# Bias load to the POOL queue, one load for W1's first block, a later parameter transpose, and the last store in partition halves

## The chip, the cores and the metric

The kernel runs on one core of one Trainium2 chip. The metric is device time in microseconds, the median of several executions. The span inside the profile is about 1.3 µs shorter than the run's time.

## The reference, cut to what matters

`x` is 2048 × 640 in bf16. The output is `g * a + (1 - g) * b`, where `g` is a sigmoid gate per row, `a` a diagonal complex state-space layer (640 states, a scan over 2048 steps, projections in and out) and `b` an MLP.

```python
h = jnp.einsum("bsd,df->bsf", x, w1) + b1     # 640 -> 1728
h = _gelu(h)
b = jnp.einsum("bsf,fd->bsd", h, w2) + b2     # 1728 -> 640
Lam_bar = jnp.exp(jnp.exp(log_dt) * Lam)
y = 2.0 * jnp.einsum("blp,dp->bld", hseq, Cmat).real + x * Dskip
```

## The kernel before

A small scheduler inside the kernel orders operations per engine by priority (a lower number goes first). What matters here is the start and the end.

At the start, SP loads a part of `x` (`xna`), W1 in row blocks, and a transposed part of `x`; ACT loads five small parameter rows into the tile `rows`. TensorE (PE) runs some dummy matmuls, transposes `xna` (line 413), starts the first 40 first-layer matmuls (line 621: five row blocks of W1 times eight column blocks), and puts in between one transpose of `rows` (line 432), which needs all five rows. The next stage begins with line 641.

```python
load("xna", "sp", "l_xna", xn[0][:, :, 0:KN * 128], x2[0:512, 0:KN * 128].rearrange(...), ["xna"], 0, ...)
for h in range(2):                                   # W1's first row block, two loads
    fs = slice(h * FW // 2, (h + 1) * FW // 2)
    load(f"w1_0{h}", "sp", f"l_w10{h}", W1sb[:, 0, fs], B_w1[0:128, fs], [("w1", 0, h)], 0.1 + h, ...)
w1load(1, "sp", 1.3)
w1load(2, "sp", 2)
xtrans(0, range(KN, KD), 3, 1.8)                     # x, transposed by the DMA
# ... cut ...
load("b1b", "act", "l_b1b", rows[RT:RT + 1, :]..., B_b1[nmain:F]..., ["b1b"], prio=-96, dur=0.4)
# ... cut ...
op("cols", "pe", 0.3, list(ROWS) + ["b1b", "ident"], [("bank", 7)], f_cols, prio=9.5)
```

At the end, the last block of 128 output rows is finished by VectorE (DVE) in two column parts, and each part is stored from SP as soon as it is ready. The last part has 256 columns (512 B per row).

```python
def f_st(hf=hf, cols=cols):
    return dma_inc("sp", nc.sync.dma_start(o2[c * 128:(c + 1) * 128, cols], osb[c % NO][:, cols]), f"stl{hf}")
op(f"stl{hf}", "sp", 0.5, [("osb", c % NO, hf)], [], f_st, prio=1000 + c, lat=2.5)
```

Of the kernel before, what the change touches and what calls it, by code (L numbers as in the profile page):

```python
# [147 lines left out]
class Prog:  # L148
# [8 lines left out]
    def op(self, name, eng, dur, reads, writes, fn, prio=None, lat=0.0, after=()):  # L157
        deps = {}
        for k in reads:
            for w in self.last_w.get(k, ()):  # L160
                deps[w.idx] = w
        for k in writes:
            for w in self.last_w.get(k, ()):
                deps[w.idx] = w
            for r in self.last_r.get(k, ()):
                deps[r.idx] = r
        for a in after:
            deps[a.idx] = a
        deps = list(deps.values())
        E = self.E  # L170

        def run(eg, deps=deps, eng=eng, fn=fn):
            E.wait(eng, *[d.done for d in deps if not (eng == "pe" and d.eng == "pe")])
            return fn()

        it = self.sch.add(name, eng, dur, deps, run, prio=prio, lat=lat)
        for k in writes:
            self.last_w[k] = [it]
            self.last_r[k] = []
        for k in reads:  # L180
            self.last_r.setdefault(k, []).append(it)
        return it


def bass_gated_mix__ssm_conv_s5__dense_activation_gelu__prompt_kernel(
# [18 lines left out]
    _, S, D = A_x.shape  # L204
# [18 lines left out]
    o2 = out[0]  # L223
    TWO_PI = 2.0 * math.pi

    with ExitStack() as es:
# [80 lines left out]
        def dma_inc(eng, ins, sem):  # L307
            SEM(sem)
            E.count.setdefault(sem, 0)
            ins.then_inc(sems[sem], 16)  # L310
            E.count[sem] += 16
            return (sem, E.count[sem])
# [7 lines left out]
        def d_mm(n):  # L320
            return n / 2400.0 + 0.004


        def load(name, eng, sem, dst, src, writes, prio, dur=0.5, lat=2.5, reads=(), **kw):
            def fn():
                return dma_inc(eng, engines[eng].dma_start(dst, src), sem)  # L326
            return op(name, eng, dur, reads, writes, fn, prio=prio, lat=lat)
# [22 lines left out]
        def w1load(k, eng, prio):  # L350
            load(f"w1_{k}", eng, f"l_w1{k}", W1sb[:, k, 0:FW], B_w1[k * 128:(k + 1) * 128, 0:FW], [("w1", k)], prio=prio, lat=2.6)
# [1 line left out]
        KN = 2  # L353

        load("xna", "sp", "l_xna", xn[0][:, :, 0:KN * 128], x2[0:512, 0:KN * 128].rearrange("(c p) d -> p c d", p=128), ["xna"], 0, dur=0.45, lat=2.0)
        for h in range(2):
            fs = slice(h * FW // 2, (h + 1) * FW // 2)
            load(f"w1_0{h}", "sp", f"l_w10{h}", W1sb[:, 0, fs], B_w1[0:128, fs], [("w1", 0, h)], 0.1 + h, dur=0.45, lat=2.0)
        w1load(1, "sp", 1.3)
        w1load(2, "sp", 2)  # L360
        xtrans(0, range(KN, KD), 3, 1.8)
# [13 lines left out]
        for i, (nm, (r0, src)) in enumerate(ROWS.items()):  # L375
            src = src.rearrange("(k p) -> k p", p=128)
            load(nm, "act", "l_" + nm, rows[r0:r0 + src.shape[0], :], src, [nm], prio=-100 + i, dur=0.4)
        load("b1b", "act", "l_b1b", rows[RT:RT + 1, :].rearrange("o (a p) -> o a p", a=2),
             B_b1[nmain:F].rearrange("(o p) -> o p", o=1).unsqueeze(1).broadcast_to([1, 2, FL]), ["b1b"], prio=-96, dur=0.4)

        def f_iota():
            inc("pool", nc.gpsimd.iota(io_i[:, :], pattern=[[1, 128]], base=0, channel_multiplier=-1))  # L382
# [48 lines left out]
        def f_cols():  # L431
            return inc("pe", nc.tensor.transpose(psC, rows[:, :], ident[:, :]))  # L432

        op("cols", "pe", 0.3, list(ROWS) + ["b1b", "ident"], [("bank", 7)], f_cols, prio=9.5)

        def f_cols1():
            return inc("dve", nc.vector.tensor_copy(out=cols[:, :], in_=psC[:, 0:RT + 1]))
# [147 lines left out]
        def pe_prio():  # L585
            ctr["pe"] += 1
            return ctr["pe"]
# [26 lines left out]
        def m1_first():  # L614
            seq = [(k, jf) for k in range(KD) for jf in range(NW)]
            seq.remove((0, NW - 1))
            seq.insert(seq.index((1, NW - 1)), (0, NW - 1))
            for k, jf in seq:

                def f_mm(jf=jf, k=k):  # L620
                    return inc("pe", nc.tensor.matmul(PS[jf][:, :], W1sb[:, k, jf * 128:(jf + 1) * 128], xT[0][:, k, :],  # L621
                                                      start=(k == 0), stop=(k == KD - 1)))

                op(f"m1_0_{jf}_{k}", "pe", d_mm(512), XK0[k] + [("w1", k) if k else ("w1", 0, jf // (NW // 2))], [("bank", jf)] ,
                   f_mm, prio=pe_prio())
            for jf in range(NW):
                ctr["bank"] += 1

                def f_ge(jf=jf):
                    return inc("act", nc.scalar.activation(Gl[0][:, jf, :], PS[jf][:, :], ACT.Gelu_apprx_tanh, bias=b1col[:, jf:jf + 1]))  # L630

                op(f"ge_0_{jf}", "act", d_act(512), [("bank", jf), "b1col"], [("gl", 0, jf)], f_ge, prio=10)

        def m1(q, j0=0):
            for jf in range(j0, NF - 1):
                bank = next_bank()

                def f_mm(jf=jf, bank=bank):
                    t = None
                    for k in range(KD):  # L640
                        t = nc.tensor.matmul(PS[bank][:, :], W1sb[:, k, jf * 128:(jf + 1) * 128], xT[q][:, k, :],  # L641
                                             start=(k == 0), stop=(k == KD - 1))
                    return inc("pe", t)

                op(f"m1_{q}_{jf}", "pe", KD * d_mm(512), XT[q] + ([("w1", 0, 0), ("w1", 0, 1)] + [("w1", k) for k in range(1, KD)] if jf < NW else [("w1", "r", int(jf * 128 >= FM))]), [("bank", bank)], f_mm, prio=pe_prio())

                def f_ge(jf=jf, bank=bank):
                    return inc("act", nc.scalar.activation(Gl[q % 2][:, jf, :], PS[bank][:, :], ACT.Gelu_apprx_tanh, bias=b1col[:, jf:jf + 1]))  # L648

                op(f"ge_{q}_{jf}", "act", d_act(512), [("bank", bank), "b1col"], [("gl", q % 2, jf)], f_ge, prio=10)  # L650
# [183 lines left out]
        def comb(c):  # L834
            q = c // 4

            def f_xg():
                return inc("dve", nc.vector.scalar_tensor_tensor(out=xg[c % 2][:, :], in0=xn[q % 2][:, c % 4, :], scalar=gcol[:, c:c + 1],  # L838
                                                                in1=dsk[:, :], op0=ALU.mult, op1=ALU.mult))

            op(f"xg{c}", "dve", d_dve(D), [("xn", q % 2, (c % 4) // 2), ("g", q), "dsk"], [("xg", c % 2)], f_xg, prio=90 + 20 * q)

            if c == NCH - 1:
                def f_half():
                    return tt(E2[c % NE][:, :], xg[c % 2][:, :], E1[c % NE][:, :], ALU.add)

                op("last", "dve", d_dve(D, 2), [("xg", c % 2), ("E1", c % NE, 0), ("E1", c % NE, 1)], [("E2", c % NE, 0), ("E2", c % NE, 1)], f_half, prio=-50)
                for hf in range(2):
                    cols = CCOLS[hf]

                    def f_fin(hf=hf, cols=cols):
                        return inc("dve", nc.vector.scalar_tensor_tensor(out=osb[c % NO][:, cols], in0=PS[cbank[hf]][:, 0:cols.stop - cols.start], scalar=gcol[:, c:c + 1],  # L852
                                                                        in1=E2[c % NE][:, cols], op0=ALU.mult, op1=ALU.add))

                    op(f"fin{hf}", "dve", d_dve(HALF), [("bank", cbank[hf]), ("E2", c % NE, 0), ("E2", c % NE, 1)], [("osb", c % NO, hf)], f_fin, prio=-60)

                    def f_st(hf=hf, cols=cols):
                        return dma_inc("sp", nc.sync.dma_start(o2[c * 128:(c + 1) * 128, cols], osb[c % NO][:, cols]), f"stl{hf}")

                    op(f"stl{hf}", "sp", 0.5, [("osb", c % NO, hf)], [], f_st, prio=1000 + c, lat=2.5)  # L860
                return

            def f_cmb():
                t = tt(osb[c % NO][:, :], xg[c % 2][:, :], E1[c % NE][:, :], ALU.add)
                E.wait("dve", t)
                return tt(osb[c % NO][:, :], osb[c % NO][:, :], E2[c % NE][:, :], ALU.add)

            op(f"cmb{c}", "dve", 2 * d_dve(D, 2), [("xg", c % 2)] + [(e, c % NE, hf) for e in ("E1", "E2") for hf in range(2)],
               [("osb", c % NO, 0), ("osb", c % NO, 1)], f_cmb, prio=-50)

            def f_st():
                return dma_inc("sp", nc.sync.dma_start(o2[c * 128:(c + 1) * 128, :], osb[c % NO][:, :]), f"st{c % NO}")

            op(f"st{c}", "sp", 0.5, [("osb", c % NO, 0), ("osb", c % NO, 1)], [], f_st, prio=1000 + c, lat=2.5)
# [69 lines left out]

        for i in range(NO):
            nc.sync.wait_ge(sems[f"st{i}"], E.count[f"st{i}"])
        for hf in range(2):
            nc.sync.wait_ge(sems[f"stl{hf}"], E.count[f"stl{hf}"])


# [26 lines left out]
```

## Time and profile before

| | before |
|---|---|
| median of 4 runs | 213.62 µs (213.25 to 213.66) |
| the profiled execution | 214.2 µs, span 212.9 µs |
| PE busy | 208.4 µs, 98% |
| start of the 41st first-layer matmul (end of the head) | 14.56 µs |
| end of the last matmul to end of the span (tail) | 2.13 µs |

The profiled execution was slower than all four timed ones.

The page of before begins with the span and the busy time of each engine:

```profile
span 212.9 us, 3113 instructions
PE 208.4 (98%) x1254; PEld 119.8 (56%) x1264; DVE 188.9 (89%) x262; ACT 111.3 (52%) x201; POOL 2.5 (1%) x10
```

The timeline of PE in before, 3 to 9 µs (start, duration, what, number of instructions merged; in brackets the idle time before and what ended it):

```profile
3.74 0.65 PE L413 MATMUL ps<-ident,xn 128*128 128x128 bf16 x8
4.64 1.04 PE L621 MATMUL ps<-xT,W1sb 128*128 128x512 bf16 x4 [0.25 <-DVE xT L419]
5.85 0.82 PE L621 MATMUL ps<-xT,W1sb 128*128 128x512 bf16 x3 [0.17 <-DMA W1sb<-in_B_w_dram]
6.92 0.61 PE L621 MATMUL ps<-xT,W1sb 128*128 128x512 bf16 x2 [0.25 <-DMA W1sb<-in_B_w_dram]
7.82 0.22 PE L432 MATMUL ps<-ident,rows 128*128 128x128 bf16 x1 [0.29 <-DMA rows<-in_B_b_dram]
7.87 1.46 PE L621 MATMUL ps<-xT,W1sb 128*128 128x512 bf16 x6
```

The matmuls come in groups of 4, 3 and 2, with three waits for a DMA between them. The idle times in brackets understate the loss, because the modelled end of a matmul overlaps the next one: four matmuls at the usual step of 0.216 µs would let the fifth start at 5.51, and it started at 5.85. By steps (from one matmul's start to the next one's), the waits are 0.34, 0.41 and 0.45 µs. The chain of waits shows the last of them as a load of 5 µs; its two rows of 128 B were issued at 2.60 µs:

```profile
2.60 5.08 DMA rows<-in_B_b_dram
7.68 0.14 issue
...
14.72 5.40 PE ps L641 x25
```

At the end, three views of before: in the timeline DVE's last piece, then the two last stores by their source line (min, median, max of the issue in ns; in µs, the time from issue to landing, which is when the DMA's last completion signal has come), then the last three ordinary stores, of 128 rows, by the tensor they write:

```profile
210.79 0.48 DVE L852 SCALAR_TENSOR_TENSOR osb<-ps,gcol,E 128x256 bf16<-128x256 f32 x1 [0.47 <-PE ps L819]
```

```profile
L858 SPq DMA_DIRECT2D out_dram<-osb x2: 332/332/333, 210.3 to 211.3; - x2
DMA to landing us min/median/max: 1.5/1.6/1.6
```

```profile
L872 SPq DMA_DIRECT2D out_dram<-osb x3: 332/332/332, 197.8 to 209.7; - x3
```

By the tile they write, one more group of the same trace, copies of 64 partitions, which my prediction had not used:

```profile
L326 SPq DMA_DIRECT2D Gt<-Gt x4: 514/602/1176, 47.7 to 50.1; - x4
```

### The profile page before, as it was taken

How to read it: one execution, taken by the hardware profiler on the slowest of the kernel's cores; microseconds unless marked ns; L12 is line 12 of the kernel's file. 1: busy time of each engine (PE TensorE's matmuls, PEld its weight loads, DVE VectorE, ACT ScalarE, POOL GpSimd, SP SyncE). 2: the span in 40 equal slices, each digit the busy share in tenths (PEclk: the TensorE clock that was granted, in tenths of full speed). 3: DMA queues.
4: the chain of work that ended last, by engine and by line, in shares of the span. 5: the costliest groups of instructions: out<-in, count | busy, mean ns of one | idle time of the engine just before them, and what ended most of it. 6: DMA issues, size and time to landing. Idle time of an engine off the chain costs nothing.

```text
span 212.9 us, 3113 instructions
## 1 busy us (share of the span) xinstructions
PE 208.4 (98%) x1254; PEld 119.8 (56%) x1264; DVE 188.9 (89%) x262; ACT 111.3 (52%) x201; POOL 2.5 (1%) x10
## 2 busy tenths in 40 slices
PE   8899999999999999999999999999999999999996
PEld 3344444444467776444466777544446777767773
DVE  2399999999999999999999959999999998999343
ACT  2389556678915324556963233555793444723330
POOL 1000000000000010000000001000000000000000
DMA  5999999998100004100000004000000000000011
GB/s 134 298 284 200 170 208 318 265 222 183 22 0 3 31 31 126 62 0 0 0 3 0 0 34 155 31 31 3 0 0 2 3 31 31 31 3 31 31 34 62
DMA packets 31434, 16.35 MB, mean 77 GB/s; under 512 B 22972, under 2 KB 30652, under 8 KB 31420
## 3 DMA queue, kind: packets, MB, share of 16 engines
q1 hardware_dynamic: 31072, 14.83, 29.2%
q0 software_dynamic: 288, 1.31, 1.9%
q8 instruction: 10, 0.16, 0.3%
q14 instruction: 4, 0.03, 0.0%
q10 hardware_dynamic: 60, 0.01, 0.0%
HBM read 7.63 MB, written 2.62 MB: 48 GB/s over the span
## 4 chain that ended last, share of the span: by engine, by line
PE 95%; DMA 2%; issue 1%; ACTq 1%; POOL 0%; DVE 0%; POOLq 0%
PE ps L771 27%; PE ps L641 22%; PE ps L819 20%; PE ps L684 20%; PE ps L621 3%; DMA rows<-in_B_b_dram 2%; PE ps L785 1%; PE ps L662 1%; ACTq L326 1%; DVE osb L852 0%; POOL io_i L382 0%; PE ps L432 0%; POOL rows L372 0%; POOL st_i L384 0%; POOL st_i L383 0%
## 5 line engine op out<-in xcount | busy, mean ns | idle before, releaser
L771 PE MATMUL ps<-W2sb,Gl 128*128 128x320 bf16 x416 | 59.2, 299 | 0.0
L771 PEld LDWEIGHTS ps<-W2sb,Gl 128*128 128x128 bf16 x416 | 40.3, 98 | 17.1 <-issue 1.1
L641 PE MATMUL ps<-xT,W1sb 128*128 128x512 bf16 x215 | 47.5, 379 | 0.3
L819 PE MATMUL ps<-CT,H 128*128 128x320 bf16 (+2 forms) x320 | 45.4, 299 | 0.0
L724 DVE TENSOR_TENSOR_SCAN W<-atab,V 128x1280 bf16<-128x1280 f32 x16 | 44.3, 2811 | 0.3
L684 PE MATMUL ps<-xT,BT 128*128 128x512 bf16 x196 | 43.1, 379 | 0.3 <-issue 0.2
L819 PEld LDWEIGHTS ps<-CT,H 128*128 128x128 bf16 x320 | 31.3, 98 | 12.2
L799 ACT ACTIVATE E<-ps,g1col 128x320 bf16<-128x320 f32 x32 | 16.3, 526 | 39.7 <-PE ps L771 26.0
L641 PEld LDWEIGHTS ps<-xT,W1sb 128*128 128x128 bf16 x220 | 21.5, 98 | 26.0
L648 ACT ACTIVATE Gl<-ps,cols 128x512 bf16<-128x512 f32 x44 | 29.6, 688 | 10.0 <-PE ps L641 10.0
L684 PEld LDWEIGHTS ps<-xT,BT 128*128 128x128 bf16 x200 | 19.5, 98 | 23.5 <-ACT Gt L670 0.4
L693 ACT ACTIVATE U<-ps 128x512 bf16<-128x512 f32 x40 | 23.8, 597 | 15.0 <-PE ps L684 14.9
L830 ACT ACTIVATE E<-ps,gcol 128x320 bf16<-128x320 f32 x30 | 15.8, 527 | 22.6 <-PE ps L819 22.6
L482 DVE TENSOR_TENSOR osb<-xg,E 128x640 bf16<-128x640 bf16 x15 | 7.3, 487 | 9.2 <-ACT E L830 8.2
L758 ACT ACTIVATE ps<-b2b 128x320 f32<-128x320 bf16 x32 | 14.1, 442 | 1.1
L838 DVE SCALAR_TENSOR_TENSOR xg<-xn,gcol,dsk 128x640 bf16<-128x640 bf16 x16 | 13.9, 883 | 0.4
L598 DVE SCALAR_TENSOR_TENSOR scr<-xn,gwb 128x640 bf16<-128x640 bf16 x16 | 13.2, 823 | 0.4
L482 DVE TENSOR_TENSOR V<-V,W 128x1280 bf16<-128x1280 bf16 x16 | 12.5, 822 | 0.3
L482 DVE TENSOR_TENSOR H<-H,V 128x1280 bf16<-128x1280 bf16 x16 | 12.5, 822 | 0.3
L482 DVE TENSOR_TENSOR V<-mr,U 128x2560 bf16<-128x2560 bf16 x8 | 11.9, 1489 | 0.2
L482 DVE TENSOR_TENSOR H<-c,W 128x2560 bf16<-128x2560 bf16 x8 | 11.9, 1489 | 0.1
L482 DVE TENSOR_TENSOR V<-s,W 128x2560 bf16<-128x2560 bf16 x8 | 11.9, 1485 | 0.0
(79 smaller groups left out, 98.5 us busy)
## 6 DMA issues: line engine op xcount, KB each, us to landing
out_dram<-osb SPq DMA_DIRECT2D x15, 160.0 KB, 1.8
W2sb<-in_B_w_dram SPq DMA_DIRECT2D x1, 2080.0 KB, 9.4
xn<-in_A_x_dram POOLq DMA_DIRECT2D x2, 640.0 KB, 4.7
W1sb<-in_B_w_dram SPq DMA_DIRECT2D x4, 256.0 KB, 4.8
xn<-in_A_x_dram SPq DMA_DIRECT2D x1, 640.0 KB, 8.0
W1sb<-in_B_w_dram SPq DMA_DIRECT2D x1, 480.0 KB, 5.7
W1sb<-in_B_w_dram SPq DMA_DIRECT2D x1, 400.0 KB, 5.8
xn<-in_A_x_dram SPq DMA_DIRECT2D x1, 384.0 KB, 6.2
```

Of the source, the lines that this page charges most:

```text
L482: return inc("dve", nc.vector.tensor_tensor(out=o, in0=a, in1=b, op=o_))
L641: t = nc.tensor.matmul(PS[bank][:, :], W1sb[:, k, jf * 128:(jf + 1) * 128], xT[q][:, k, :], start=(k == 0), stop=(k == KD - 1))
L648: return inc("act", nc.scalar.activation(Gl[q % 2][:, jf, :], PS[bank][:, :], ACT.Gelu_apprx_tanh, bias=b1col[:, jf:jf + 1]))
L684: t = nc.tensor.matmul(PS[bank][:, :], BT[:, ci, kd, k * 128:(k + 1) * 128], xT[q][:, kd, :], start=(kd == 0), stop=(kd == KD - 1))
L693: return inc("act", nc.scalar.activation(dst, src, ACT.Copy, scale=1.0 if ci == 0 else -1.0))
L724: t = inc("dve", nc.vector.tensor_tensor_scan(out=g[:, ci, :], data0=a, data1=v[:, ci, :], initial=0.0, op0=ALU.mult, op1=ALU.add))
L758: return inc("act", nc.scalar.activation(PS[bank][:, 0:HALF], b2b[:, cols], ACT.Copy))
L771: t = nc.tensor.matmul(PS[bank][:, 0:HALF], Gl[q % 2][:, jf, t4 * 128:(t4 + 1) * 128], W2sb[:, jf, cols], start=False, stop=False, skip_gr ...
L799: return inc("act", nc.scalar.activation(E1[c % NE][:, cols], PS[bank][:, 0:HALF], ACT.Copy, scale=g1col[:, c:c + 1]))
L819: t = nc.tensor.matmul(PS[bank][:, 0:n], H[b % NHB][:, ci, k, s * 128:(s + 1) * 128], CT[:, ci, k, cols], start=(i == 0), stop=(i == 2 * K ...
L830: return inc("act", nc.scalar.activation(E2[c % NE][:, cols], PS[bank][:, 0:HALF], ACT.Copy, scale=gcol[:, c:c + 1]))
L838: return inc("dve", nc.vector.scalar_tensor_tensor(out=xg[c % 2][:, :], in0=xn[q % 2][:, c % 4, :], scalar=gcol[:, c:c + 1], in1=dsk[:, :] ...
```

## The change

Four edits. The small bias row moves from ACT's queue to POOL's. The transpose of the parameter rows goes two matmuls later. W1's first row block comes in one load instead of two (one issue less on SP). The last store is cut into two halves of 64 partitions, one from SP and one from ACT.

```diff
-        for h in range(2):
-            fs = slice(h * FW // 2, (h + 1) * FW // 2)
-            load(f"w1_0{h}", "sp", f"l_w10{h}", W1sb[:, 0, fs], B_w1[0:128, fs], [("w1", 0, h)], 0.1 + h, ...)
+        w1load(0, "sp", 1)
 ...
-        load("b1b", "act", "l_b1b", rows[RT:RT + 1, :]..., ["b1b"], prio=-96, dur=0.4)
+        load("b1b", "pool", "l_b1b", rows[RT:RT + 1, :]..., ["b1b"], prio=-50, dur=1.0)
 ...
-        op("cols", "pe", 0.3, ..., f_cols, prio=9.5)
+        op("cols", "pe", 0.3, ..., f_cols, prio=11.5)
 ...
-                    def f_st(hf=hf, cols=cols):
-                        return dma_inc("sp", nc.sync.dma_start(o2[c * 128:(c + 1) * 128, cols], osb[c % NO][:, cols]), f"stl{hf}")
+                    for h, eng in enumerate(("sp",) if hf == 0 else ("sp", "act")):
+                        n = 128 if hf == 0 else 64
+                        def f_st(hf=hf, cols=cols, h=h, n=n, eng=eng):
+                            return dma_inc(eng, engines[eng].dma_start(o2[c * 128 + h * n:c * 128 + (h + 1) * n, cols],
+                                                                       osb[c % NO][h * n:(h + 1) * n, cols]), f"stl{hf}{h}")
```

The rest adapts dependencies and the final waits.

More of the change, by code (lines that the diff above doesn't have):

```diff
@@ L355, in bass_gated_mix__ssm_conv_s5__dense_activation_gelu__prompt_kernel @@
         load("xna", "sp", "l_xna", xn[0][:, :, 0:KN * 128], x2[0:512, 0:KN * 128].rearrange("(c p) d -> p c d", p=128), ["xna"], 0, dur=0.45, lat=2.0)
-        for h in range(2):
-            fs = slice(h * FW // 2, (h + 1) * FW // 2)
-            load(f"w1_0{h}", "sp", f"l_w10{h}", W1sb[:, 0, fs], B_w1[0:128, fs], [("w1", 0, h)], 0.1 + h, dur=0.45, lat=2.0)
+        w1load(0, "sp", 1)
         w1load(1, "sp", 1.3)
@@ L377, in bass_gated_mix__ssm_conv_s5__dense_activation_gelu__prompt_kernel @@
             load(nm, "act", "l_" + nm, rows[r0:r0 + src.shape[0], :], src, [nm], prio=-100 + i, dur=0.4)
-        load("b1b", "act", "l_b1b", rows[RT:RT + 1, :].rearrange("o (a p) -> o a p", a=2),
-             B_b1[nmain:F].rearrange("(o p) -> o p", o=1).unsqueeze(1).broadcast_to([1, 2, FL]), ["b1b"], prio=-96, dur=0.4)
+        load("b1b", "pool", "l_b1b", rows[RT:RT + 1, :].rearrange("o (a p) -> o a p", a=2),
+             B_b1[nmain:F].rearrange("(o p) -> o p", o=1).unsqueeze(1).broadcast_to([1, 2, FL]), ["b1b"], prio=-50, dur=1.0)
         def f_iota():
@@ L432, in f_cols @@
             return inc("pe", nc.tensor.transpose(psC, rows[:, :], ident[:, :]))
-        op("cols", "pe", 0.3, list(ROWS) + ["b1b", "ident"], [("bank", 7)], f_cols, prio=9.5)
+        op("cols", "pe", 0.3, list(ROWS) + ["b1b", "ident"], [("bank", 7)], f_cols, prio=11.5)
         def f_cols1():
@@ L622, in f_mm @@
                                                       start=(k == 0), stop=(k == KD - 1)))
-                op(f"m1_0_{jf}_{k}", "pe", d_mm(512), XK0[k] + [("w1", k) if k else ("w1", 0, jf // (NW // 2))], [("bank", jf)] ,
+                op(f"m1_0_{jf}_{k}", "pe", d_mm(512), XK0[k] + [("w1", k)], [("bank", jf)] ,
                    f_mm, prio=pe_prio())
@@ L643, in f_mm @@
                     return inc("pe", t)
-                op(f"m1_{q}_{jf}", "pe", KD * d_mm(512), XT[q] + ([("w1", 0, 0), ("w1", 0, 1)] + [("w1", k) for k in range(1, KD)] if jf < NW else [("w1", "r", int(jf * 128 >= FM))]), [("bank", bank)], f_mm, prio=pe_prio())
+                op(f"m1_{q}_{jf}", "pe", KD * d_mm(512), XT[q] + ([("w1", k) for k in range(KD)] if jf < NW else [("w1", "r", int(jf * 128 >= FM))]), [("bank", bank)], f_mm, prio=pe_prio())
                 def f_ge(jf=jf, bank=bank):
@@ L855, in comb @@
                     op(f"fin{hf}", "dve", d_dve(HALF), [("bank", cbank[hf]), ("E2", c % NE, 0), ("E2", c % NE, 1)], [("osb", c % NO, hf)], f_fin, prio=-60)
-                    def f_st(hf=hf, cols=cols):
-                        return dma_inc("sp", nc.sync.dma_start(o2[c * 128:(c + 1) * 128, cols], osb[c % NO][:, cols]), f"stl{hf}")
-                    op(f"stl{hf}", "sp", 0.5, [("osb", c % NO, hf)], [], f_st, prio=1000 + c, lat=2.5)
+                    for h, eng in enumerate(("sp",) if hf == 0 else ("sp", "act")):
+                        n = 128 if hf == 0 else 64
+                        def f_st(hf=hf, cols=cols, h=h, n=n, eng=eng):
+                            return dma_inc(eng, engines[eng].dma_start(o2[c * 128 + h * n:c * 128 + (h + 1) * n, cols], osb[c % NO][h * n:(h + 1) * n, cols]), f"stl{hf}{h}")
+                        op(f"stl{hf}{h}", eng, 0.5, [("osb", c % NO, hf)], [], f_st, prio=1000 + c, lat=2.5)
                 return
@@ L946, in bass_gated_mix__ssm_conv_s5__dense_activation_gelu__prompt_kernel @@
             nc.sync.wait_ge(sems[f"st{i}"], E.count[f"st{i}"])
-        for hf in range(2):
-            nc.sync.wait_ge(sems[f"stl{hf}"], E.count[f"stl{hf}"])
+        for n in ("stl00", "stl10", "stl11"):
+            nc.sync.wait_ge(sems[n], E.count[n])
 _INS = ['A_x', 'A_Lambda_re', 'A_Lambda_im', 'A_B_re', 'A_B_im', 'A_C_re', 'A_C_im', 'A_log_dt', 'A_Dskip', 'B_x', 'B_w1', 'B_b1', 'B_w2', 'B_b2', 'gate_w']
```

## The prediction

> **What bounds the kernel now.** TensorE. The page gives PE 208.4 us busy of 212.9 us (98%), and the chain of waits is PE for 95% of the span. Read by start-to-start steps (0.216 us for a 512-column matmul), PE never waits between 7.87 us and the last matmul's end at 210.6 us. So only two places can pay: the head before 7.87 us and the tail after 210.6 us. A head gain passes to the end one for one, since everything later has slack: the weights for the second projection land at 16.3 and 20.8 us and are used from 20.1 and about 24; W2 lands by 40.9 and is used from 58; each scan result is ready over 8 us before its projection.
>
> **The head, from the timeline and the DMA landings.** The first-layer matmuls start at 4.64 us (behind VectorE's copies of the PE transposes). Then PE waits three times: 0.34 us for W1's second half-block (landed 5.81), 0.42 us for W1's block 1 (landed 6.87), 0.45 us for the parameter transpose, whose last input is the single-row bias (issued from ACT at 2.60, landed only at 7.68). Sum 1.21 us. From 7.87 us, 31 first-layer matmuls run without a break. The next data deadline is the transposed x blocks: landed 9.05, needed 9.38, so only 0.33 us slack.
>
> **The change, costed.**
> 1. Bias load from POOL: takes a 0.68 us issue from ACT, which is idle, and leaves the queue where two 128 B rows took 5.1 us. POOL starts it after its iotas (about 1.4 us). A later 640 KB POOL load moved its first packet 1.6 us after the instruction's start; I estimate landing at 4 to 6 us.
> 2. Transpose two matmuls later: 0.43 us more tolerance. With 1, the 0.45 us wait disappears. Its other rows landed by 5.21.
> 3. One W1 load: saves one SP issue (0.54 us), so W1 blocks 1 and 2 and the x transpose are issued 0.54 us earlier. But the first four matmuls lose their early start (first half landed 4.03) and wait for all 256 KB: estimate 5.2 us, range 4.5 to 5.8. The two W1 waits become mainly one wait before the first matmul. The packets show a near-empty stretch from 3.4 to 4.5 us (about 50 GB/s, some packets over 0.7 us); whether it hits the joint load or block 1 is my main uncertainty.
> 4. Store halves: the last store takes 1.53 us from issue to landing, of which its packets take 0.36. The Trainium skill ("DMA: Bandwidth & Descriptors", Rules for kernel authors) says not to bother with two transfers to disjoint partition halves, because both use the same 16 DMA engines. The trace agrees on the size available: 96 KB took 1.6 us, 64 KB 1.5. Gain 0 to 0.1 us.
>
> **Sum.** A start at 5.2 us with no further wait ends the first 40 matmuls at about 13.9 us, against 14.56: 0.65 us gain. If the x transpose still lands at 9.05, they end at 14.29: 0.27 us. I expect about 0.4 in the head, 0.03 in the tail: **213.2 us, 80% range 212.6 to 213.75**. Chances: faster by over 2% 0.01, within 2% 0.98, slower 0.01.
>
> **Right or wrong would show as:** no PE wait for the bias; first first-layer matmul later than 4.64, but the matmul group up to the second stage ending before 14.5; SP issuing the x transpose near 2.7 us; last store still about 1.5 us to landing; the middle unchanged in length.
>
> **What would make it wrong:** POOL's row landing after 7 us; the whole W1 block landing after 5.8 (gain gone); the x transpose becoming PE's wait, keeping the gain under 0.3; or the DMA gap vanishing, gaining over 0.8.

## The result, and the profile after

The changed kernel took 214.06 µs (4 runs, 213.78 to 214.18) against 213.62 µs. The ratio is 1.0023, interval 1.0005 to 1.0040. The change is slower by about 0.4 to 0.5 µs: within 2%, but on the wrong side, and outside the predicted range.

The page of after, its first lines:

```profile
span 212.8 us, 3123 instructions
PE 209.0 (98%) x1264; PEld 120.3 (57%) x1264; DVE 189.2 (89%) x262; ACT 111.3 (52%) x201; POOL 3.0 (1%) x11
```

PE's timeline in after, 3 to 9 µs, then the end of the head in its chain of waits:

```profile
3.88 0.88 PE L411 MATMUL ps<-ident,xn 128*128 128x128 bf16 x8 [0.17 <-DMA xn<-in_A_x_dram]
4.87 2.72 PE L619 MATMUL ps<-xT,W1sb 128*128 128x512 bf16 x11
7.43 0.22 PE L430 MATMUL ps<-ident,rows 128*128 128x128 bf16 x1
7.48 1.83 PE L619 MATMUL ps<-xT,W1sb 128*128 128x512 bf16 x7
```

```profile
14.07 5.40 PE ps L639 x25
```

The head did what was planned. Eleven matmuls run almost without a break, the transpose does not wait for the bias (landed 4.88 µs), and the next stage comes 0.65 µs earlier in the chain than before (14.07 against 14.72). By steps, two short waits are left, 0.16 µs for W1's block 1 and 0.15 µs for the transposed `x`. By start, the 41st matmul begins at 13.90 µs against 14.56.

The tail in after, in the timeline (DVE's last piece, the two halves) and by source line:

```profile
210.14 0.48 DVE L850 SCALAR_TENSOR_TENSOR osb<-ps,gcol,E 128x256 bf16<-128x256 f32 x1 [0.47 <-PE ps L817]
210.65 0.51 SPq L859 DMA_DIRECT2D out_dram<-osb  x1
210.65 0.55 ACTq L859 DMA_DIRECT2D out_dram<-osb  x1
```

```profile
L859 SPq DMA_DIRECT2D out_dram<-osb x2: 333/420/507, 209.7 to 210.7; - x2
L859 ACTq DMA_DIRECT2D out_dram<-osb x1: 553/553/553, 210.7 to 210.7; - x1
DMA to landing us min/median/max: 1.6/1.8/2.1
```

Here is the loss. A half issues in 0.51 or 0.55 µs where the whole store took 0.33, and the later half lands 2.1 µs after its issue instead of 1.5. From the last matmul's end to the end of the span it is 2.68 µs against 2.13. The head's gain of 0.66 µs and the tail's loss of 0.56 leave the two profiled spans nearly equal (212.8 and 212.9). But the profiled execution of before was slow for its kernel, so most executions had less head to win and the same tail to lose.

### The profile page after: what moved, and what is told of

It reads as the page before. It is cut to its first block, busy times and chain, and to the rows that moved or that the text cites. A ratio compares the mean times of both kernels' runs of the same rounds, so it can differ in the third digit from the quotient of the medians.

```text
span 212.8 us, 3123 instructions
## 1 busy us (share of the span) xinstructions
PE 209.0 (98%) x1264; PEld 120.3 (57%) x1264; DVE 189.2 (89%) x262; ACT 111.3 (52%) x201; POOL 3.0 (1%) x11
## 4 chain that ended last, share of the span: by engine, by line
PE 97%; DMA 1%; DVE 0%; issue 0%
PE ps L769 27%; PE ps L639 22%; PE ps L817 20%; PE ps L682 20%; PE ps L619 4%; DMA xn<-in_A_x_dram 1%; PE ps L783 1%; PE ps L660 1%; DVE xT L417 0%; DVE osb L850 0%; PE ps L411 0%; PE ps L430 0%
## 5 line engine op out<-in xcount | busy, mean ns | idle before, releaser
L639 PE MATMUL ps<-xT,W1sb 128*128 128x512 bf16 x220 | 48.1, 379 | 0.0
L682 PE MATMUL ps<-xT,BT 128*128 128x512 bf16 x200 | 43.8, 379 | 0.0
L836 DVE SCALAR_TENSOR_TENSOR xg<-xn,gcol,dsk 128x640 bf16<-128x640 bf16 x16 | 13.9, 883 | 0.4
L480 DVE TENSOR_TENSOR W<-mi,U 128x2560 bf16<-128x2560 bf16 x8 | 11.9, 1485 | 0.0
```

Of the source, the lines that this page charges most:

```text
L480: return inc("dve", nc.vector.tensor_tensor(out=o, in0=a, in1=b, op=o_))
L639: t = nc.tensor.matmul(PS[bank][:, :], W1sb[:, k, jf * 128:(jf + 1) * 128], xT[q][:, k, :], start=(k == 0), stop=(k == KD - 1))
L682: t = nc.tensor.matmul(PS[bank][:, :], BT[:, ci, kd, k * 128:(k + 1) * 128], xT[q][:, kd, :], start=(kd == 0), stop=(kd == KD - 1))
L836: return inc("dve", nc.vector.scalar_tensor_tensor(out=xg[c % 2][:, :], in0=xn[q % 2][:, c % 4, :], scalar=gcol[:, c:c + 1], in1=dsk[:, :] ...
```

## The experiments

**Theory A:** halving the last store costs 0.55 µs in every execution; the head gains less than the pair of profiles suggests, because the profiled before was unlucky. **Rival B:** the tail is neutral, the profile of before was typical, and something outside the span got dearer. The twelve runs came in three groups, each beside its own runs of before on the same chip (medians 213.88, 213.87 and 213.90 µs).

### before_again: another look at the kernel before

```diff
+# the kernel before, unchanged
```

> The kernel before, unchanged. Theory A (the profiled execution of before had an unlucky head: its profile-run time was 214.2 us against a median of 213.62): this one gives about 213.6 us, spans near 212.3 us, and a profile in which the first 40 first-layer matmuls end at 14.0 to 14.3 us instead of 14.56. Rival B (the profile was typical, and something outside the span got dearer in the changed kernel): spans near 212.9 us and the head ending at 14.5 us again.

It took 213.63 µs, ratio 0.9995 (0.9982 to 1.0007), spans 212.1 to 212.8 µs. The head ended at 14.34 µs. Theory A holds on the spans: before's executions range over 0.7 µs, and the spans are 1.3 µs below the times, as for the changed kernel, so nothing moved outside the span. The head end was slightly beyond what I had named (14.0 to 14.3). The chain of waits of this run shows a head with a different cause:

```profile
4.71 3.05 PE ps L622 x9
7.76 0.06 PE ps L433
...
14.51 5.40 PE ps L642 x25
```

Nine matmuls took 3.05 µs here and eleven took 2.72 in after, yet no wait for a DMA is in this chain. The steps tell: the first five matmuls come 0.38 to 0.43 µs apart and the later ones 0.216. PE was still at half rate. (The granted clock that the profile lists reads 1.0 over these slow matmuls too, so it does not show this; the steps do.) The Trainium skill ("TensorE: Matmul & The Clock Gate", Part 1) says that PE starts at half its clock and is released after a busy window of about 3.4 µs that runs freely, so that the point varies from run to run. Full steps of 512 columns are 0.427 and 0.216 µs, and transposes of 128 columns come 0.107 or 0.056 µs apart. The release came by 3.9 µs in the profile of before, at most 3.1 µs after PE's first matmul and so a little under that window, and between 6.3 and 6.7 µs in this one. This late release hides the waits for data, as the slow matmuls ask for it later: here the fifth one started at 6.35 µs and its half of W1's block had landed at 5.53, while in before PE was ready for it at 5.51 and it landed at 5.81. The data also came earlier in this run than in before (the bias at 7.02 against 7.68 µs).

### tail_undone: the changed head, the last store whole

```diff
-                    for h, eng in enumerate(("sp",) if hf == 0 else ("sp", "act")):   # halves
+                    def f_st(hf=hf, cols=cols):                                       # one store from SP, as before
```

> The changed kernel with the last store whole again, from SP. Theory A (the halved store costs 0.55 us, because the two halves go through the issue one after the other and land later): 213.5 us, last store 1.55 us from issue to landing, ratio to before 0.9985 to 1.0000. Rival B (the tail is neutral): 214.0 us, ratio 1.002.

213.50 µs (213.39 to 213.69), ratio 0.9985 (0.9973 to 0.9997). The head ended at 13.82 µs and the tail took 2.13 µs. Theory A holds. The three head edits together gain about 0.3 µs. The five executions have spans of 212.1 to 212.4, those of before beside it 212.2 to 212.8; that they scatter less is not shown, as those of w1_halves_kept below, with nearly the same head, range over 211.8 to 212.4.

### tail_alone: before with only the halved store

```diff
-                    def f_st(hf=hf, cols=cols):
+                    for h, eng in enumerate(("sp",) if hf == 0 else ("sp", "act")):
```

> The kernel before with only the last store in halves. Theory A: 0.5 to 0.6 us slower than before, 214.15 us, ratio 1.0025; in the profile both last issues take over 0.5 us and the later half lands 2.1 us after its issue. Rival B: 213.6 us, ratio 1.000.

214.32 µs, ratio 1.0029 (1.0015 to 1.0042), so 0.6 µs slower. The tail took 2.71 µs. Theory A holds and rival B falls. The stores of this run:

```profile
L861 SPq DMA_DIRECT2D out_dram<-osb x2: 333/422/510, 209.6 to 210.6; - x2
L861 ACTq DMA_DIRECT2D out_dram<-osb x1: 564/564/564, 210.6 to 210.6; - x1
```

The head of this run, the same instructions as before, ended at 13.81 µs. So the same head ended at 14.56, 14.34 and 13.81 µs in three profiles.

### w1_halves_kept: bias from POOL and the later transpose, W1 in two loads, store whole

```diff
 (before, with:)
-        load("b1b", "act", ..., prio=-96, dur=0.4)
+        load("b1b", "pool", ..., prio=-50, dur=1.0)
-        op("cols", ..., f_cols, prio=9.5)
+        op("cols", ..., f_cols, prio=11.5)
```

> Before with the bias load from POOL and the transpose two matmuls later, but W1's first block in two loads and the last store whole. If the joint W1 load cost time by its late start, this is faster than tail_undone: 213.2 us. If the joint load helped by freeing an issue, it is slower: 213.7 us. If neither matters, both give the same within 0.15 us.

213.49 µs (213.16 to 213.68), ratio 0.9983 (0.9971 to 0.9995), head end 13.96 µs. It ties with tail_undone, so the joint W1 load neither helps nor hurts beside the other two edits. Both versions are faster than before, and so faster than the changed kernel.

### tail_act_whole: is ACT's queue the slow part?

```diff
-  ... nc.sync.dma_start(...)          # both last parts from SP
+  eng = "sp" if hf == 0 else "act"    # the very last part whole from ACT
```

> Before, with the last store whole but issued from ACT instead of SP. If ACT's queue is the slow part of the halved store: time from the last matmul's end to the end of the span over 2.3 us (2.12 in before), landing over 1.75 us after issue. If the slow part is two issues competing for one generator: 2.1 to 2.2 us and an issue of about 0.33 us, time as before (ratio 1.000).

The tail took 2.18 µs, 0.05 more than from SP; ratio 1.0004 (0.9989 to 1.0020). ACT's queue is a little slower (issue 0.39 µs, landing 1.58), which is a tenth of the loss.

```profile
L859 ACTq DMA_DIRECT2D out_dram<-osb x1: 391/391/391, 210.9 to 210.9; - x1
```

### tail_sp_halves: the halves one after the other from SP

```diff
-                    for h, eng in enumerate(("sp",) if hf == 0 else ("sp", "act")):
+                    for h, eng in enumerate(("sp",) if hf == 0 else ("sp", "sp")):
```

> Before, with both halves of 64 partitions from SP, one after the other. The first half runs with no rival, so it shows the 64-partition shape by itself. If the shape is slow: its issue takes about 0.5 us and its first packet comes over 1.1 us after the issue, as in the changed kernel. If only the competition is slow: issue about 0.33 us or less and first packet 0.83 us after it; then the second half ends about 0.3 us later than a whole store would. Time 0.3 to 0.6 us above before.

214.92 µs, ratio 1.0049 (1.0031 to 1.0066), tail 3.06 µs.

```profile
L861 SPq DMA_DIRECT2D out_dram<-osb x3: 333/505/597, 209.8 to 211.3; - x3
```

Of these, 333 ns is the part of 128 partitions, 505 the first half and 597 the second. The first half had no rival when it was issued, and still took 505 ns, sent its first packet 1.16 µs after its issue instead of 0.83, and landed after 1.80 µs instead of 1.53. So the 64-partition shape is slow by itself: it has half the bytes and half the packets and lands 0.27 µs later. The loss is larger than I had written down (1.0 µs against 0.3 to 0.6), as the second half pays it again.

### tail_col_halves: two queues, but 128 partitions each

```diff
-  o2[c*128 + h*n : c*128 + (h+1)*n, cols], osb[c % NO][h*n:(h+1)*n, cols]     # 64 rows, 256 columns
+  o2[c*128 : (c+1)*128, cc],               osb[c % NO][:, cc]                 # 128 rows, 128 columns
```

> Before, with the last store cut by columns instead (all 128 partitions, 128 columns each) from SP and ACT. If two queues issuing at once is what costs, both issues take over 0.45 us and the loss is 0.4 to 0.7 us as with partition halves. If the 64-partition shape costs, the loss is under 0.2 us.

213.72 µs, ratio 0.9991 (0.9976 to 1.0007), tail 2.25 µs.

```profile
L859 SPq DMA_DIRECT2D out_dram<-osb x2: 332/332/333, 209.7 to 210.7; - x2
L859 ACTq DMA_DIRECT2D out_dram<-osb x1: 383/383/383, 210.7 to 210.7; - x1
```

Two queues at once, with the same bytes in each part as in the change, cost 0.12 µs of tail, not 0.56. The issues are at their usual 0.33 and 0.38 µs. The shape is the larger part of the loss. In neither way of halving do the two queues start together. Counted from DVE's last write, the starts of packets in the records:

| last store | first packet | last packet | end of the span |
|---|---|---|---|
| whole, from SP (before) | 0.86 | 1.19 | 1.60 |
| change: SP's 64 rows | 1.19 | 1.46 | |
| change: ACT's 64 rows | 1.46 | 1.74 | 2.16 |
| column halves: SP's 128 rows | 0.86 | 1.13 | |
| column halves: ACT's 128 rows | 0.98 | 1.25 | 1.73 |

In the change the first packet of ACT's half starts 3 ns after the last packet of SP's half does (14 ns in tail_alone): one queue runs after the other. The column halves overlap for 0.15 µs. The Trainium skill ("Perfetto Trace Analysis", DMA Instruction — HWDGE) says that the descriptor generator is locked for one DMA at a time and that SP and ACT (by its note) share it. The order of the packets in the change agrees with that. The overlap of the column halves and the lengths of the issues do not show it: ACT's issue took 0.55 µs beside SP's 0.51, begun 4 ns apart, so it did not wait out SP's whole issue, and ACT's took 0.06 µs longer than SP's for the whole store too (0.39 against 0.33). The records do not show the generator itself, so why the queues take turns stays open. By the packets, 0.33 µs of the loss comes before the first packet, from the shape, and 0.27 µs from ACT's half starting after SP's; the shorter run of packets gives 0.05 back. Of the 0.27, an estimated 0.06 is ACT's queue itself: the whole store's first packet came after 0.92 µs from ACT and 0.86 from SP.

### rows_pool: all parameter rows from POOL

The load queue moves only about 100 GB/s between 3.75 and 4.75 µs in the trace of tail_undone, in a stretch where ACT's small loads go through the same DMA engines. This run takes them from ACT.

```diff
 (tail_undone, with:)
-            load(nm, "act", ..., prio=-100 + i, dur=0.4)      # four parameter rows
+            load(nm, "pool", ..., prio=-50 + i, dur=0.7)
-        op("cols", ..., f_cols, prio=11.5)
+        op("cols", ..., f_cols, prio=14.5)
```

> The changed head with all five parameter rows loaded from POOL, the transpose later (after 18 matmuls), the last store whole. If the small loads from ACT cause the near-empty stretch of the load queue at 3.4 to 4.5 us, it goes: block 1 of W1 lands near 5.5 instead of 6.4 us and the transposed x near 7.8 instead of 8.6 us, and the first 40 matmuls can end near 13.4 us when the clock warms early: 213.1 us. If something else causes it, the landings stay within 0.2 us and the time is 213.5 us; if POOL's rows land after 8.6 us, PE waits for them and it is slower.

214.67 µs (213.99 to 215.04), ratio 1.0039 (1.0023 to 1.0055): slower. The mechanism showed in part. The stretch filled to between 207 and 246 GB/s (by quarters of a microsecond), W1's block 1 landed at 5.60 µs (6.42 in tail_undone) and the transposed `x` at 8.07 (8.58). But POOL takes 0.5 to 0.7 µs per load, the last row landed at 7.83, and the transpose ran only at 8.99. The gelu waits for those columns: its first one started at 13.46 µs, against 12.51 in tail_undone, and PE, which needs the first gelu's bank, started the next stage 0.25 µs late, 0.14 µs after that gelu ended. It had also waited 0.34 µs for the transposed `x` and 0.23 µs for the copy of the columns. The profiled execution was the fastest of six; what the slower ones lost beyond that was not seen.

### bias_pool_alone, cols_late_alone, w1_one_alone: each head edit by itself

```diff
-        load("b1b", "act", ..., prio=-96, dur=0.4)        # bias_pool_alone
+        load("b1b", "pool", ..., prio=-50, dur=1.0)

-        op("cols", ..., f_cols, prio=9.5)                 # cols_late_alone
+        op("cols", ..., f_cols, prio=11.5)

-        for h in range(2): load(f"w1_0{h}", ...)          # w1_one_alone
+        w1load(0, "sp", 1)
```

> Before with only the bias load moved to POOL. If the head's gain comes from the bias row landing late in some executions: the bias lands at 4.2 to 4.9 us instead of 6.9 to 7.7, PE never waits for it, and the time is 0.2 to 0.4 us under before (ratio 0.998 to 0.999), with a narrower spread of spans. If the gain comes from the later transpose or the joint load: ratio 1.000.

> Before with only the parameter transpose two matmuls later. It gives the late bias 0.43 us more time, so where the bias lands by 7.2 us the wait goes: ratio 0.998 to 0.999 if the bias wait is all there is to the gain. Ratio 1.000 if the wait is merely replaced by the one for the transposed x.

> Before with only W1's first block in one load. My prediction's reading (fewer issues bring the later loads forward by 0.5 us) gives the transposed x landing near 8.0 us and ratio 0.998. The reading from the runs so far (landings are set by the filled load queue, not by when SP issues): the transposed x lands at 8.4 to 8.7 us as before and the ratio is 1.000, 0.999 to 1.001.

| edit alone | median µs | ratio to before (95%) | bias landed | transposed `x` landed | waits left in the profile (by steps) | head end |
|---|---|---|---|---|---|---|
| bias from POOL | 213.65 | 0.9996 (0.9980 to 1.0011) | 4.27 | 8.63 | 0.33 W1 block 1, 0.18 `x` | 13.87 |
| transpose later | 213.87 | 0.9999 (0.9985 to 1.0013) | 7.66 | 9.01 | 0.53 W1 block 1, 0.05 bias, 0.13 `x` | 14.25 |
| W1 block in one load | 213.85 | 0.9998 (0.9984 to 1.0011) | 7.33 | 8.69 | 0.47 bias | 14.21 |

None of the three gains clearly by itself, where I had expected the bias edit to. Each removes one wait and leaves another. The intervals still allow 0.3 to 0.4 µs for each, so these times do not say how the 0.3 µs of the joint head is divided. The last one does settle a step of the prediction: the issue of the transposed `x` came at 2.80 instead of 3.27 µs, and it landed at 8.69 µs, no earlier than in the heads with two loads (8.26 to 9.05).

### b1_pool: a try at a better version

```diff
 (tail_undone, with:)
-            load(nm, "act", ...)
+            load(nm, "pool" if nm == "b1a" else "act", ...)    # the 13-row bias too
```

> The changed head with the 13-row bias load on POOL too, the last store whole: a try at a version that beats both kernels. If the ACT rows slow the load queue, block 1 of W1 lands near 6.0 and the transposed x near 8.3 us, the transpose is not late (rows by 6.5 us), and the time is 213.2 to 213.4 us, ratio 0.997 to 0.998. If the rows cost nothing there: as tail_undone, ratio 0.9985.

213.56 µs, ratio 0.9988 (0.9975 to 1.0002). W1's block 1 landed at 6.63 µs and the transposed `x` at 8.73, not earlier. Moving this load brings nothing over tail_undone; which of ACT's rows thin the load queue stays open.

### The heads side by side

| head | profiles | head end, µs | bias landed, µs | first-layer matmuls whose step PE's lower rate stretched |
|---|---|---|---|---|
| as before | before, before_again, tail_alone, tail_act_whole, tail_sp_halves, tail_col_halves | 14.56, 14.34, 13.81, 14.11, 14.05, 13.94 (mean 14.14) | 7.68, 7.02, 6.93, 7.23, 7.17, 7.01 | 0, 5, 3, 2, 2, 3 |
| bias from POOL, transpose later | after, tail_undone, w1_halves_kept | 13.90, 13.82, 13.96 (mean 13.89) | 4.88, 4.45, 4.22 | 0, 0, 3 |

The mean gain is 0.24 µs, near the 0.3 that the times give. The pair of profiles that I first compared shows 0.66.

The landing of the bias tells more than PE's rate. In before, tail_alone, tail_act_whole and tail_sp_halves, with 0, 3, 2 and 2 slow steps, the transpose started 0.14 µs after the bias had landed and the head ended 6.88 µs after it, so the landing alone set the head's end. In tail_col_halves it was 6.93 µs, and only in before_again, with five slow steps, did PE's rate decide (7.32 µs). What made the profile of before slow is thus its late bias: 7.68 µs, against 6.93 to 7.23 in the other five. So moving the bias can pay mainly in the executions where it lands late; in tail_alone the old head ended as early as the changed ones. Of the three waits that I first read, those for W1 appear in none of the other five profiles, and the one for the bias in two (0.33 µs each). Why the bias lands later in some executions is not shown.

## Why the prediction was wrong

- **The failed step is point 4, the store halves.** I gave it "Gain 0 to 0.1 us". It lost 0.56 µs in the trace, in both kernels that have it (tail 2.68 and 2.71 against 2.13), and 0.6 by the times of tail_alone. I costed it by bytes, from two stores of 128 partitions (96 KB in 1.6 µs, 64 KB in 1.5), which says nothing about another shape. The 64-partition copies in the trace of before, with issues of 514 to 1176 ns beside 332 for the stores, could have warned me. They would not have proved it, as loads of W1 into 128 partitions in that trace have issues of 424 to 1183 ns. I also took "they share the same engines" for the worst case, which would be no gain. The experiments show two costs: the shape (first packet 0.33 µs later even without a rival) and, with that shape, the second queue starting 0.27 µs after the first.
- **The head's size (about 0.4) was a little high but in range.** Point 1 was right: the bias landed at 4.2 to 5.0 µs when it alone, or first, came from POOL, and PE never waited for it again. Point 2 was right as a tolerance: alone, it left 0.05 µs of wait for a bias that landed at 7.66. With the tail whole, the head gains 0.3 µs (ratio 0.9985, 0.9973 to 0.9997). That I did not take the full 0.65 µs of the sum was right, but for another reason than I gave: the base was one slow execution. That the head of after ended at 13.90, the 13.9 of the sum's first line, was luck: it started 0.33 µs earlier than assumed and then lost 0.31 in two waits that this line left out.
- **Point 3 half failed.** The issue moved forward by 0.5 µs as said, and the first matmul was not held back to 5.2 µs: the joint block landed at 4.3 to 4.7, beside DVE's copies, so the start was 4.7 to 4.9. But the earlier issue did not bring the transposed `x` forward (8.6 to 8.7 µs with one load). It did become a short wait for PE, 0.15 µs, as I had named among the risks.
- **What I did not see:** the landing of the bias and PE's rate in the first 7 µs both change from run to run. The profile of before had the latest bias of six and the earliest release, so it shows the largest waits for data. Whether the two hang together is not shown.
- **Sum:** on the first chip 213.62 − 0.3 + 0.56 would be 213.9; measured 214.06, within the scatter. With the store left whole, the ratio of tail_undone on 213.62 gives 213.3, inside the predicted range and near its middle.

Open: why a DMA of 64 partitions takes longer to issue than one of 128. The runs show that it does and not the cause.

## What to carry to other kernels

Cost a DMA by its shape, from a record of the same shape in the same trace, and not by its bytes: at the end of a kernel, one store of 128 partitions beat two halves on two queues. Where an effect is below half a microsecond, look at several executions before naming what bounds the start, since one profile can show waits that most executions do not have. Saving an issue need not bring data forward: here the transposed `x`, issued 0.47 µs earlier, landed no earlier, most likely because the queue was filled with loads before it (argued, not shown).

The best versions tried were w1_halves_kept and tail_undone (213.5 µs): keep the bias on POOL and the later transpose, and leave the last store whole.

## What the Trainium skill lacked or had wrong

- "DMA: Bandwidth & Descriptors", Rules for kernel authors, says of two transfers to disjoint partition halves not to bother, because they serialize. The direction is right, but it reads as no gain; here it cost 0.56 µs on a store of 64 KB, and 0.94 with both halves from SP. In the change the packets did go one queue after the other.
- No page I read has the cost of the partition count: in the last store, an issue of 64 partitions from SP took 505 to 510 ns and sent its first packet 1.16 to 1.17 µs after the issue; one of 128 partitions took 333 ns and 0.83 µs.
- The same rule covers partition halves only and says nothing of halves by columns: these, with 128 partitions each from SP and ACT, cost 0.12 µs of tail, and their packets overlapped for 0.15 µs.
- "TensorE: Matmul & The Clock Gate", Part 1, gives ±500 ns for the run-to-run variation of the release, though it also says that the number of slow matmuls varies. Here the release came by 3.9 µs in one profile and after 6.3 µs in another of the same kernel, with PE's first matmul at 0.78 µs in both: at most 3.1 µs after it and at least 5.5, so at least 2.4 µs apart.
